# Second sums made in the bank of the first, evictions ahead of statistics, and output stores on another queue

## The chip, the cores and the metric

The kernel runs on one core of one Trainium2 chip. Its time is the device time of an execution in microseconds. Before the change it was 1675.91 us, the median of three runs (1675.52 to 1676.21). One more execution was taken by the hardware profiler; all positions below are microseconds from the start of its span.

## What is computed

Four layers on a sequence of 2048 tokens with 512 features: spectral, attention, spectral, attention. Each adds its result to x. The two spectral layers are alike, and so are the two attention layers.

```python
def spectral(x, w_r, w_i):
    X = rfft2(x.astype(float32))           # over tokens s and features d
    return irfft2(X * (w_r + 1j * w_i), s=(2048, 512)).astype(bfloat16)

def attention(x, wq, wk, wv, wo):          # 32 heads of 16, one shared k and v
    q = (x @ wq).reshape(B, S, 32, 16).transpose(0, 2, 1, 3)
    k, v = x @ wk, x @ wv
    p = softmax(einsum("bhqd,bkd->bhqk", q, k) / 4)
    return einsum("bhqk,bkd->bhqd", p, v).transpose(0, 2, 1, 3).reshape(B, S, 512) @ wo

for layer in (spectral, attention, spectral, attention):
    x = x + layer(layernorm(x))
```

## The kernel before, in words

**State.** `x_sb` and its normalised copy `xn_sb` stay in SBUF as 16 blocks of 128 tokens by 512 features, block (r, t) with r and t from 0 to 3. `k = 4t + r` numbers the blocks in the closing loops.

**Spectral layer** (`spectral_layer`, L201). The transforms are matrix products with tables of cosines and sines. `over_s` sums over tokens into `G` (for the third layer most of it is done at the end of the attention layer before, by `sequence`), DVE combines the four residues t into `X` (L231 to L242), and `over_d` (L262) sums over features. For a half c of the frequencies it is called with sign 0 and with sign 1: the first result is a + b, the second a - b, where a is the sum with the cosines and b with the sines, per real and imaginary part and for two blocks of frequencies. Each call has four results, and each result is eight matmuls into a PSUM bank of its own (L275) and an eviction by ACT into `F`, which lies in the buffer of `xn_sb` (L279). The table `DT` holds cos, sin and -sin. Then DVE multiplies by the weights (`times_w`, L293 to L295), combines the signs (`combine`, L299 to L318) into `st`, and TensorE goes back over d (L367) and over s (L379). A few frequencies left over go another way (`extras`, L320): small matmuls with `DT` (L325, L326), one copy by ACT (L329), a row of small operations on POOL (L335 to L353), and a copy by DVE into `st[0]` (L410). In the first layer alone `prepare_w` brings the weights into the layout `WT` (TensorE L151 and L153, ACT L158, DVE L160), and POOL copies the raw `wq` (L882).

**Order of the spectral stage** (L400 to L424): sums over d for c = 0, sign 0 and 1; weights; sums for c = 1, sign 0; extras; products of c = 0; sums for c = 1, sign 1; back over d; and so on.

**Attention layer** (`attention_layer`, L497). A written-out loop of steps feeds ACT's exponentials (L669), a share of them made on DVE (L693, L699), and the sums over keys (L681). The function `chain` makes each of TensorE, ACT, DVE and POOL keep the order in which the program text issues; the SP queue, which issues every DMA, is not among those four.

**Its end** (L742 to L823). The output product of the 16 blocks runs in triples of blocks, each triple in a PSUM tile of three banks (two such tiles exist, pool `psc`), and four last blocks which wait for the last group of heads. `finish` (L650) adds a block to x: where `with_x` holds, TensorE adds x by a product with the identity and ACT copies the result (L653); else DVE adds (L655). In the layer between (`nxt` set), `statistics` (L742, L743) and `normal` (L749 to L758) make the next layer's normalised blocks, and `sequence` starts its sums over tokens (L192), evicted by ACT (L197). In the last layer each finished block is stored to DRAM (L891).

The last group's denominators take a way of their own: `evict` copies the sums to SBUF (L584), writes one row per head to DRAM (`d`, L586) and reads it back spread over partitions (`den`, L588); `invert` takes the reciprocal (L592), writes it (L594) and reads it back broadcast, in four DMAs (`rb`, L597). Then POOL multiplies (`od`, L619), and TensorE adds the last product of the four last blocks.

Of the kernel before, what the change touches and what calls it, by code (L numbers as in the profile page):

```python
# [11 lines left out]
P = 128  # L12
# [6 lines left out]
NC = 4  # L19
# [23 lines left out]
def host_tables():  # L43
# [24 lines left out]
    tabs["DT"] = bf(np.stack([np.cos(angd), np.sin(angd), -np.sin(angd)], axis=2))  # L68
# [132 lines left out]
def spectral_layer(nc, tc, tabs, shared, lnpool, x_sb, xn_sb, WT, WX, aw, nxt, loads):  # L201
# [5 lines left out]
    with (tc.tile_pool(name="workA", bufs=1) as work,  # L207
# [54 lines left out]
        def over_d(c, sign, by_half):  # L262
            pss = [None] * 4
            for bs in ((0, 1), (2, 3)) if by_half else ((0, 1, 2, 3),):
                for i in range(4):
                    fb, comp = divmod(i, 2)
                    if pss[i] is None:
                        pss[i] = psum.tile([P, 512], F32, tag="pa", name=f"fd{i}")
                    for b in bs:
                        for part in range(2):  # L270
                            if part == comp:
                                w = 0
                            else:
                                w = 1 if (part == 1) == (sign == 0) else 2
                            nc.tensor.matmul(pss[i], lhsT=DT[:, b, w, 128 * fb:128 * fb + 128],  # L275
                                             rhs=X[:, b, part, c, :, :].rearrange("p k j -> p (k j)"),
                                             start=(b == 0 and part == 0), stop=(b == 3 and part == 1))
                    if bs[-1] == 3:
                        nc.scalar.copy(out=F[:, 8 * c + 4 * comp + 2 * fb + sign, :], in_=pss[i])  # L279

        Z = work.tile([P, 2, 2, 2, 512], BF, name="Z")
        V = work.tile([P, 2, 2, 2, 4, 128], BF, name="V")
# [117 lines left out]
        over_d(0, 0, True)  # L400
        over_d(0, 1, False)
# [4 lines left out]
        over_d(1, 0, False)  # L406
# [4 lines left out]
        over_d(1, 1, False)  # L411
# [85 lines left out]
def attention_layer(nc, tc, tabs, shared, lnpool, x_sb, xn_sb, aw, prep, nxt, store):  # L497
    with ExitStack() as ctx:
# [151 lines left out]
        def finish(k, ps, with_x):  # L650
            t, r = divmod(k, 4)
            if with_x:
                nc.scalar.copy(out=x_sb[:, r, t, :], in_=ps)  # L653
            else:
                nc.vector.tensor_tensor(out=x_sb[:, r, t, :], in0=ps, in1=x_sb[:, r, t, :], op=ALU.add)  # L655
            if store is not None:
                store(r, t)
# [64 lines left out]
        mv, n_x = {}, 1 if nxt is None else 2  # L722

        def triple(i):
            ps = psc.tile([P, 3, 512], F32, tag="sc", name="tri")
            for j in range(3):
                outproj(3 * i + j, ps[:, j, :], j < n_x)
            return ps

        def triple_out(i, ps):  # L730
            for j in range(3):
                finish(3 * i + j, ps[:, j, :], j < n_x)

        def statistics(ks):
            if nxt is None:
                return
            for k in ks:
                t, r = divmod(k, 4)
                if r == 0:
                    mv[t] = lnpool.tile([P, 4, 2], F32, tag="ln_mv4", bufs=4, name="mv")  # L740
                stats = lnpool.tile([P, 6], F32, tag="ln_stats", bufs=4)
                nc.vector.bn_stats(stats, x_sb[:, r, t, :])  # L742
                nc.vector.bn_aggr(mv[t][:, r, :], stats)  # L743

        def normal(t):
            if nxt is None:
                return
            rstd = lnpool.tile([P, 4], F32, tag="ln_rstd4", bufs=4)
            nc.scalar.activation(out=rstd, in_=mv[t][:, :, 1], func=ACT.Sqrt, bias=tabs["eps"], scale=1.0)  # L749
            nc.vector.reciprocal(rstd, rstd)  # L750
            nb = lnpool.tile([P, 4], F32, tag="ln_nb4", bufs=4)
            nc.vector.scalar_tensor_tensor(out=nb, in0=mv[t][:, :, 0], scalar=-1.0, in1=rstd, op0=ALU.mult, op1=ALU.mult)
            for r, eng in ((0, nc.scalar), (1, nc.gpsimd), (2, nc.vector), (3, nc.vector)):
                x_ap, xn_ap = x_sb[:, r, t, :], xn_sb[:, r, t, :]
                if eng is nc.scalar:
                    eng.activation(out=xn_ap, in_=x_ap, func=ACT.Identity, bias=nb[:, r:r + 1], scale=rstd[:, r:r + 1])
                else:
                    eng.tensor_scalar(out=xn_ap, in0=x_ap, scalar1=rstd[:, r:r + 1], scalar2=nb[:, r:r + 1],  # L758
                                      op0=ALU.mult, op1=ALU.add)
# [34 lines left out]
        normal(0)  # L794
        triple_out(2, p2)
        normalise(NG - 1, o, rb)
        if nxt is not None:
            nxt["load"](2)
        p3 = triple(3)
        statistics((6, 7, 8))  # L800
        normal(1)
        triple_out(3, p3)
# [5 lines left out]
        for i in range(4):  # L808
            outproj(12 + i, pf[i], i % 2 == 0)
        statistics((9, 10, 11))  # L810
        normal(2)
        q0 = sequence(0)
        sequence_out(q0)
        for i in range(4):
            outproj(12 + i, pf[i], False, last_group=True)
# [5 lines left out]
        normal(3)  # L821
# [7 lines left out]
def full_kernel(ctx, tc, A_x, A_w_r, A_w_i, B_x, B_wq, B_wk, B_wv, B_wo, out,  # L829
# [39 lines left out]
    def late_loads(work):  # L869
        wq_raw = work.tile([P, NC, D], BF, name="wq_raw")  # L870
# [19 lines left out]
    def store(r, t):  # L890
        nc.sync.dma_start(out=out_v[:, r, t, :], in_=x_sb[:, r, t, :])  # L891
# [62 lines left out]
```

## Time and profile before

| | |
|---|---|
| median of three runs | 1675.91 us |
| the profiled execution | 1673.17 us |
| its span, first to last instruction | 1671.4 us |
| mean granted TensorE clock | 0.977 |
| busy in the span: PE, DVE, ACT, POOL | 85%, 93%, 90%, 9% |
| DMA: moved, share of 16 engines (hardware queue) | 40.26 MB, 7.7% |
| first spectral layer and attention's inputs | about 0 to 132 us |
| attention loop of layer 2 | about 132 to 820 us |
| end of layer 2, third layer | about 820 to 957 us |
| attention loop of layer 4, tail | about 957 to 1645 us, 1645 to 1671.4 us |

A row of a timeline has the start, the time from first to last of a run of like instructions, the engine, the line, the operation, output <- inputs, shapes, how many, and in brackets the idle time of that engine before it with what ended it. "SPq" is the SP queue, which issues DMAs. The chain view has the start, the length and what the path that ended last was doing.

### The profile page before, as it was taken

The page shows a single profiled execution, that of the slowest core. Times are in us where ns is not written, and L with a number is a line of the kernel's source. Part 1 is how long each engine was busy: PE and PEld are TensorE (multiplying, and loading weights), DVE is VectorE, ACT ScalarE, POOL GpSimd, SP SyncE. Part 2 cuts the span into 40 slices and gives each one's busy share as a digit, 9 for nine tenths or more (in the row PEclk, how much of TensorE's full clock was granted, in tenths as well). Part 3 has the DMA queues.
Part 4 walks back from the last instruction along what each step waited for, and adds up shares of the span by engine and source line. Part 5 has one row for each costly group of instructions (what it writes and reads, how often), then busy time and mean ns, then how long its engine had stood idle before and what let it go on. Part 6 is the DMA issues. An engine that isn't in the chain of part 4 may idle for free.

```text
span 1671.4 us, 32246 instructions
## 1 busy us (share of the span) xinstructions
PE 1421.6 (85%) x12756; PEld 459.7 (28%) x12756; DVE 1551.7 (93%) x2796; ACT 1505.6 (90%) x1250; POOL 158.4 (9%) x264
## 2 busy tenths in 40 slices
PE   7889888888888888888988798888888888888887
PEld 2331222222222222222333322222222222222222
DVE  6877999999999999999878689999999999999994
ACT  4358999999999999999843699999999999999994
POOL 3210000000000000000111100000000000000000
PEclk9896999999999999999999789999999999999999
DMA  7000000000000010000020000000000000000002
GB/s 276 2 1 4 14 16 17 17 16 17 17 17 16 16 29 16 17 17 28 24 70 1 1 8 17 17 16 17 17 16 16 17 15 15 14 16 17 16 17 65
DMA packets 47880, 40.26 MB, mean 24 GB/s; under 512 B 30832, under 2 KB 36208, under 8 KB 47472
## 3 DMA queue, kind: packets, MB, share of 16 engines
q1 hardware_dynamic: 47728, 38.19, 7.7%
q8 instruction: 100, 1.64, 0.4%
q14 instruction: 52, 0.43, 0.1%
HBM read 33.04 MB, written 3.15 MB: 22 GB/s over the span
## 4 chain that ended last, share of the span: by engine, by line
DVE 39%; ACT 24%; PE 18%; issue 17%; DMA 1%; POOL 1%; SPq 0%; POOLq 0%; DVEq 0%; ACTq 0%
ACT e L669 23%; DVE t_new L693 15%; DVE s_new L699 12%; PE pv_new L681 6%; PE dv L569 3%; PE sc L569 2%; DVE o L584 2%; DVE qt L446 2%; PE fd L275 2%; DVE qt L447 2%; PE ps L192 1%; DVE stats L125 1%; PE ps L367 1%; PE ps L379 1%; DVE den L592 1%
## 5 line engine op out<-in xcount | busy, mean ns | idle before, releaser
L669 ACT ACTIVATE e<-sc 128x1536 bf16<-128x1536 f32 (+1 forms) x1028 | 1386.4, 1526 | 16.0 <-PE sc L569 15.5
L693 DVE TENSOR_SCALAR t_new<-dv 128x512 int16<-128x512 f32 x1016 | 695.0, 684 | 35.8 <-PE sc L569 14.5
L699 DVE TENSOR_SCALAR s_new<-t_new 128x2048 int16<-128x2048 int16 x1016 | 698.3, 688 | 0.0
L569 PE MATMUL dv<-qt,KT 32*128 32x512 bf16 x1016 | 389.2, 383 | 121.8 <-DVE t_new L693 114.0
L569 PE MATMUL sc<-qt,KT 32*128 32x512 bf16 x3080 | 421.6, 389 | 36.5 <-ACT e L669 3.2
L681 PE MATMUL pv_new<-s_new,vaug 128*32 128x512 bf16 x4064 | 412.0, 393 | 27.0 <-DVE qt L446 27.0
L681 PE MATMUL pv_new<-e,vaug 128*32 128x512 bf16 x3080 | 408.7, 385 | 0.4 <-ACT e L669 0.4
L569 PEld LDWEIGHTS <-KT 32*128 32x128 bf16 x4096 | 201.2, 91 | 730.1 <-issue 714.9
L681 PEld LDWEIGHTS <-vaug 128*32 128x32 bf16 x7144 | 135.6, 94 | 276.1 <-issue 262.5
L625 POOL TENSOR_TENSOR ot_new<-o,rb 128x176 bf16<-128x176 f32 (+1 forms) x96 | 55.7, 582 | 706.8 <-DVE s_new L699 649.9
L625 POOL TENSOR_TENSOR od<-o,rb 128x176 bf16<-128x176 f32 (+1 forms) x90 | 49.6, 551 | 597.6 <-DVE s_new L699 597.6
L441 PE MATMUL ps<-xT,wq_sb 128*128 128x512 bf16 x256 | 66.3, 381 | 10.8 <-DVE o L584 10.8
L275 PE MATMUL fd<-X,tab_DT 128*128 128x512 bf16 x256 | 56.1, 379 | 2.8 <-DVE X L242 2.8
L279 ACT CAST xn_sb<-fd 128x512 bf16<-128x512 f32 x32 | 18.8, 586 | 40.7 <-PE fd L275 40.7
L446 DVE CAST qt<-ps 128x512 bf16<-128x512 f32 x64 | 44.2, 691 | 0.8 <-PE ps L441 0.8
L584 DVE COPY o<-pv_new 128x512 f32<-128x512 f32 x64 | 43.8, 684 | 0.1
L367 PE MATMUL ps<-tab_PS,st 128*128 128x512 bf16 x128 | 32.8, 416 | 13.0 <-DVE st L315 12.0
L373 ACT CAST U<-ps 128x512 bf16<-128x512 f32 x24 | 14.1, 587 | 29.8 <-PE ps L367 29.8
L125 DVE BATCH_NORM_STATS2 stats<-x_sb 128x6 f32<-128x512 bf16 x48 | 31.8, 677 | 7.2 <-ACT x_sb L383 3.7
L441 PEld LDWEIGHTS <-wq_sb 128*128 128x128 bf16 x256 | 24.6, 96 | 39.7 <-issue 16.0
L275 PEld LDWEIGHTS <-tab_DT 128*128 128x128 bf16 x256 | 24.8, 98 | 32.8 <-issue 3.6
L379 PE MATMUL ps<-U,IT 128*128 128x512 bf16 x128 | 33.2, 379 | 0.0
(133 smaller groups left out, 567.2 us busy)
## 6 DMA issues: line engine op xcount, KB each, us to landing
rb<-d SPq DMA_DIRECT2D x256, 64.0 KB
FT<-const_FT SPq DMA_DIRECT2D x8, 512.0 KB
IT<-const_IT SPq DMA_DIRECT2D x8, 512.0 KB
x_sb<-in_A_x_dram SPq DMA_DIRECT2D x4, 512.0 KB
out_dram<-x_sb SPq DMA_DIRECT2D x16, 128.0 KB
ot_new<-od SPq DMA_DIRECT2D x120, 16.0 KB
wr_raw<-in_A_w_r_dram SPq DMA_DIRECT2D x1, 1028.0 KB
wi_raw<-in_A_w_i_dram SPq DMA_DIRECT2D x1, 1028.0 KB
```

The costliest lines, as they stand in the source:

```text
L275: nc.tensor.matmul(pss[i], lhsT=DT[:, b, w, 128 * fb:128 * fb + 128], rhs=X[:, b, part, c, :, :].rearrange("p k j -> p (k j)"), start=(b = ...
L367: nc.tensor.matmul(ps, lhsT=st[c][:, t, vec, q, fb, :], rhs=PS[:, fb, w, :], start=(k == 0), stop=(k == 3))
L379: nc.tensor.matmul(ps, lhsT=IT[:, t, part, c, r * P:(r + 1) * P], rhs=U[:, t, part, c, :], start=(k == 0), stop=(k == 3 and r % 2 == 1))
L441: nc.tensor.matmul(ps, lhsT=wq_sb[:, c, hg, :], rhs=xTq[qb][:, c, :], start=(c == 0), stop=(c == NC - 1))
L446: nc.vector.tensor_copy(out=qt, in_=ps)
L569: nc.tensor.matmul(dst, lhsT=KT[hs, kc * P:(kc + 1) * P], rhs=QT[g][hs, :], start=True, stop=True)
L584: nc.vector.tensor_copy(out=o, in_=pv.pop(g))
L625: pace(nc.gpsimd.tensor_tensor(out=dst[:, a:b], in0=o[:, a:b], in1=rb[:, a:b], op=ALU.mult))
L669: nc.scalar.activation(out=e[:, 0:na, :], in_=sc[:, 0:na, :], func=ACT.Exp, scale=SCALE)
L681: nc.tensor.matmul(pv[g][32 * h:32 * h + 32, :], lhsT=vaug[:, max(j, 0), kc, :], rhs=rhs, start=(first_pv[(g, h)] == u), stop=(last_pv[(g, ...
L693: nc.vector.tensor_scalar(out=tb[(g, kc // 4)][:, kc % 4, :], in0=dv, scalar1=T_MUL, scalar2=T_ADD, op0=ALU.mult, op1=ALU.add)
L699: image[0] = nc.vector.tensor_scalar(out=s_new, in0=tb[(g, b)], scalar1=0.5, scalar2=16384.0 + PH_OFF[j], op0=ALU.mult, op1=ALU.add)
```

## The change

1. `over_d` makes both sums of a pair. The four banks of the first sums are kept; for the second, TensorE adds four products with -2 sin or 2 sin into the bank from which ACT has just copied the first. `DT` holds five tables instead of three, and `V` and `wq_raw` now share a buffer, one waiting for the other.
2. At the end of the attention layer that has a next one, the evictions of triple 2 come ahead of `normal(0)`, those of triple 3 ahead of the statistics of triple 2 and of `normal(1)`; `normal` is split so that the square root on ACT can be issued earlier than the rest; the fourth block's normalisation goes from DVE to ACT.
3. In the last layer no block of the first twelve goes by way of the identity product and ACT: DVE adds them all. Of the 16 stores, 14 are issued on POOL's queue, and two (blocks 13 and 15) on SP's.

```diff
@@ host_tables
-    tabs["DT"] = bf(np.stack([np.cos(angd), np.sin(angd), -np.sin(angd)], axis=2))
+    tabs["DT"] = bf(np.stack([np.cos(angd), np.sin(angd), -np.sin(angd), 2 * np.sin(angd), -2 * np.sin(angd)], axis=2))
@@ before L259, after L259
 
         F = xn_sb.rearrange("p r t d -> p (r t) d")
 
-        def over_d(c, sign, by_half):
+
+        def over_d(c, by_half):
             pss = [None] * 4
+
+            def add(i, b, part, w, start, stop):
+                fb = i // 2
+                nc.tensor.matmul(pss[i], lhsT=DT[:, b, w, 128 * fb:128 * fb + 128],
+                                 rhs=X[:, b, part, c, :, :].rearrange("p k j -> p (k j)"),
+                                 start=start, stop=stop, skip_group_check=True)
+
+            def out(i, sign):
+                fb, comp = divmod(i, 2)
+                nc.scalar.copy(out=F[:, 8 * c + 4 * comp + 2 * fb + sign, :], in_=pss[i])
+
             for bs in ((0, 1), (2, 3)) if by_half else ((0, 1, 2, 3),):
                 for i in range(4):
-                    fb, comp = divmod(i, 2)
+                    comp = i % 2
                     if pss[i] is None:
                         pss[i] = psum.tile([P, 512], F32, tag="pa", name=f"fd{i}")
                     for b in bs:
                         for part in range(2):
-                            if part == comp:
-                                w = 0
-                            else:
-                                w = 1 if (part == 1) == (sign == 0) else 2
-                            nc.tensor.matmul(pss[i], lhsT=DT[:, b, w, 128 * fb:128 * fb + 128],
-                                             rhs=X[:, b, part, c, :, :].rearrange("p k j -> p (k j)"),
-                                             start=(b == 0 and part == 0), stop=(b == 3 and part == 1))
+                            add(i, b, part, 0 if part == comp else 1 + comp, b == 0 and part == 0, b == 3 and part == 1)
                     if bs[-1] == 3:
-                        nc.scalar.copy(out=F[:, 8 * c + 4 * comp + 2 * fb + sign, :], in_=pss[i])
+                        out(i, 0)
+            yield
+            for i in range(4):
+                comp = i % 2
+                for b in range(4):
+                    add(i, b, 1 - comp, 4 - comp, False, b == 3)
+                out(i, 1)
 
         Z = work.tile([P, 2, 2, 2, 512], BF, name="Z")
-        V = work.tile([P, 2, 2, 2, 4, 128], BF, name="V")
+        V = work.tile([P, 2, 2, 2, 4, 128], BF, tag="V", bufs=1, name="V")
@@ before L397, after L409
         slots()
-        over_d(0, 0, True)
-        over_d(0, 1, False)
+        f0 = over_d(0, True)
+        next(f0)
+        next(f0, None)
         if raw:
             prepare_w(nc, tabs, psum, raw, WT, WX)
         times_w(0, 0, lo)
         times_w(0, 0, hi)
-        over_d(1, 0, False)
+        f1 = over_d(1, False)
+        next(f1)
         rx = extras()
         times_w(0, 1, both)
         combine(st[0], both)
         v.tensor_copy(out=st[0].rearrange("p t v q m j -> p t (v q) m j")[:, :, 1:3, :, 0], in_=rx)
-        over_d(1, 1, False)
+        next(f1, None)
         back_d(0)
         times_w(1, 0, both)
@@ before L654, after L668
             else:
                 nc.vector.tensor_tensor(out=x_sb[:, r, t, :], in0=ps, in1=x_sb[:, r, t, :], op=ALU.add)
             if store is not None:
-                store(r, t)
+                store(r, t, nc.sync if t == T - 1 and r % 2 == 1 else nc.gpsimd)
@@ before L719, after L733
-        mv, n_x = {}, 1 if nxt is None else 2
+        mv, n_x = {}, 0 if nxt is None else 2
@@ before L744, after L758
 
         def normal(t):
             if nxt is None:
-                return
+                return lambda: None
             rstd = lnpool.tile([P, 4], F32, tag="ln_rstd4", bufs=4)
             nc.scalar.activation(out=rstd, in_=mv[t][:, :, 1], func=ACT.Sqrt, bias=tabs["eps"], scale=1.0)
-            nc.vector.reciprocal(rstd, rstd)
-            nb = lnpool.tile([P, 4], F32, tag="ln_nb4", bufs=4)
-            nc.vector.scalar_tensor_tensor(out=nb, in0=mv[t][:, :, 0], scalar=-1.0, in1=rstd, op0=ALU.mult, op1=ALU.mult)
-            for r, eng in ((0, nc.scalar), (1, nc.gpsimd), (2, nc.vector), (3, nc.vector)):
-                x_ap, xn_ap = x_sb[:, r, t, :], xn_sb[:, r, t, :]
-                if eng is nc.scalar:
-                    eng.activation(out=xn_ap, in_=x_ap, func=ACT.Identity, bias=nb[:, r:r + 1], scale=rstd[:, r:r + 1])
-                else:
-                    eng.tensor_scalar(out=xn_ap, in0=x_ap, scalar1=rstd[:, r:r + 1], scalar2=nb[:, r:r + 1],
-                                      op0=ALU.mult, op1=ALU.add)
+
+            def rest():
+                nc.vector.reciprocal(rstd, rstd)
+                nb = lnpool.tile([P, 4], F32, tag="ln_nb4", bufs=4)
+                nc.vector.scalar_tensor_tensor(out=nb, in0=mv[t][:, :, 0], scalar=-1.0, in1=rstd,
+                                               op0=ALU.mult, op1=ALU.mult)
+                for r, eng in ((0, nc.scalar), (1, nc.gpsimd), (2, nc.vector), (3, nc.scalar)):
+                    x_ap, xn_ap = x_sb[:, r, t, :], xn_sb[:, r, t, :]
+                    if eng is nc.scalar:
+                        eng.activation(out=xn_ap, in_=x_ap, func=ACT.Identity, bias=nb[:, r:r + 1],
+                                       scale=rstd[:, r:r + 1])
+                    else:
+                        eng.tensor_scalar(out=xn_ap, in0=x_ap, scalar1=rstd[:, r:r + 1], scalar2=nb[:, r:r + 1],
+                                          op0=ALU.mult, op1=ALU.add)
+            return rest
 
         def sequence(first):
             if nxt is None:
@@ before L791, after L810
         rb = invert(den)
         p2 = triple(2)
         statistics((3, 4, 5))
-        normal(0)
         triple_out(2, p2)
+        rest = normal(0)
+        p3 = triple(3)
+        rest()
         normalise(NG - 1, o, rb)
         if nxt is not None:
             nxt["load"](2)
-        p3 = triple(3)
+        triple_out(3, p3)
         statistics((6, 7, 8))
-        normal(1)
-        triple_out(3, p3)
+        rest = normal(1)
         if nxt is not None:
             nxt["load"](3)
         ps_a = psc.tile([P, 3, 512], F32, tag="sc", name="tri")
@@ before L807, after L827
         pf = [ps_a[:, 0, :], ps_a[:, 1, :], ps_a[:, 2, :], ps_b]
         for i in range(4):
             outproj(12 + i, pf[i], i % 2 == 0)
+        rest()
         statistics((9, 10, 11))
-        normal(2)
         q0 = sequence(0)
         sequence_out(q0)
+        rest = normal(2)
+        rest()
         for i in range(4):
             outproj(12 + i, pf[i], False, last_group=True)
         for i in range(4):
@@ before L818, after L840
         q1 = sequence(3)
         statistics((12, 13, 14, 15))
         sequence_out(q1)
-        normal(3)
+        rest = normal(3)
+        rest()
         for first in (6, 9):
             q2 = sequence(first)
             sequence_out(q2)
@@ before L867, after L890
         return raw
 
     def late_loads(work):
-        wq_raw = work.tile([P, NC, D], BF, name="wq_raw")
+        wq_raw = work.tile([P, NC, D], BF, tag="V", bufs=1, name="wq_raw")
         nc.sync.dma_start(out=wq_raw, in_=B_wq.rearrange("(c p) j -> p c j", p=P))
         wk_v = B_wk.rearrange("(c p) j -> p c j", p=P)
         for i in range(8):
@@ before L887, after L910
     out_v = out_flat.rearrange("(r p t) d -> p r t d", r=R, p=P, t=T)
     n_layers = len(layers)
 
-    def store(r, t):
-        nc.sync.dma_start(out=out_v[:, r, t, :], in_=x_sb[:, r, t, :])
+    def store(r, t, eng):
+        eng.dma_start(out=out_v[:, r, t, :], in_=x_sb[:, r, t, :])
```

## The prediction, made before the changed kernel was run

> **What bounds the kernel now.** I read the busy shares first, then the chain that ended last, then the timelines of the stretches that the change touches. The chain spends most of the span in the two attention loops (about 132 to 820 us and 957 to 1645 us), which the change leaves alone. What it can move lies in four stretches, each with its own limit: the spectral stage of the first layer, the end of the first attention layer, the spectral stage of the third layer, and the tail.
>
> In the first stage, the chain (start, length, what) goes from TensorE's sums over d straight to the preparation of W:
> ```profile
> 29.41 13.97 PE fd L275 x64
> 43.38 0.03 PE ps L151
> ...
> 43.88 3.69 DVE WT L160 x6
> ```
> DVE stood idle for 4.15 us before 43.88, so TensorE sets the time there. But not by much: DVE's earlier work ended late, beside a POOL copy.
> ```profile
> 33.68 1.86 DVE L250 TENSOR_TENSOR uv<-G 128x4 f32<-128x4 bf16 x1
> ...
> 37.35 1.88 DVE L252 SCALAR_TENSOR_TENSOR Y<-uv,G 128x4 bf16<-128x4 f32 x1
> ...
> 39.57 0.17 DVE L257 COPY Y<-Y 128x16 bf16<-128x16 bf16 x1
> ```
> ```profile
> 31.22 7.98 POOL L882 COPY wq_sb<-wq_raw 128x2048 bf16<-128x2048 bf16 x2 [12.91 <-DMA wq_raw<-in_B_wq_dram]
> ```
> Two tiny DVE operations of 128x4 took 1.86 and 1.88 us where their like take 0.15 and 0.17; both end with one of the two POOL copies (35.5 and 39.2).
>
> In the third layer DVE waits three times; in brackets, its idle time and what ended it:
> ```profile
> 876.38 0.69 DVE L293 TENSOR_TENSOR m<-xn_sb,WT 128x1024 bf16<-128x1024 bf16 x1 [1.44 <-ACT xn_sb L279]
> ...
> 878.17 0.69 DVE L294 TENSOR_TENSOR m<-xn_sb,WT 128x1024 bf16<-128x1024 bf16 x1 [1.09 <-ACT xn_sb L279]
> ...
> 892.48 0.21 DVE L410 COPY st<-rx 128x16 bf16<-128x16 bf16 x1 [1.05 <-POOL rx L353]
> ```
> The first two are for the second sums' evictions, the third for POOL's small operations, which start after TensorE's extra sums at 884. From 892.48 to the next TensorE stage at 905.90 the chain is DVE alone.
>
> At the end of the first attention layer the chain runs through statistics on DVE and evictions on ACT:
> ```profile
> 853.91 0.31 ACT rstd L749
> ...
> 854.72 0.81 ACT xn_sb L756
> 855.53 2.94 ACT G L197 x6
> 858.47 0.04 issue
> 858.51 1.90 PE ps L192 x8
> ```
> In the tail, one denominator travels d, den, d, rb through DRAM on the SP queue, between stores of the output:
> ```profile
> 1651.18 0.55 SPq L586 DMA_DIRECT2D d<-o  x1
> 1652.71 1.06 SPq L891 DMA_DIRECT2D out_dram<-x_sb  x2
> 1653.86 0.38 SPq L588 DMA_DIRECT2D den<-d  x1
> ...
> 1660.18 1.79 SPq L597 DMA_DIRECT2D rb<-d  x4
> 1662.02 7.01 SPq L891 DMA_DIRECT2D out_dram<-x_sb  x6
> ...
> 1663.98 1.26 POOL L619 TENSOR_TENSOR od<-o,rb 128x512 bf16<-128x512 f32 x1 [21.24 <-DMA rb<-d]
> ```
> Everything after waits for od at 1665.24.
>
> **Part 1, sums over d.** A pair took 64 matmuls and takes 48: 16 fewer, four pairs in all. A second sum must wait until ACT has read the first from its bank. That wait has cover: the eviction lasts 0.59 us, and 12 or more matmuls (2.6 us) lie between it and the next write to that bank. I cost it at nothing.
>
> *First layer.* A matmul takes 13.97 / 64 = 0.218 us, so W's preparation starts 16 x 0.218 = 3.5 us earlier: DVE could cast at 43.88 - 3.5 = 40.4. Next late is DVE itself. The table DT grows from 768 to 1280 KB; the DMA engines were full (392 to 423 GB/s between 10 and 25 us), so all loads queued behind DT land 0.52 MB / 0.41 MB per us = 1.3 us later, among them wq_raw, for which POOL's copies wait. If the two held DVE operations move with them, DVE is free at 39.74 + 1.3 = 41.0. Gain 43.9 - 41.0 = 2.8 (3.5 if they don't). W's raw tables were there before 31 us, so 1.3 us more is covered. After that DVE is gapless to the end of the stage, so the second pair's 16 matmuls bring nothing. [...] The buffer that V now shares with wq_raw adds a wait on POOL's copies; they end at about 40.5 and V is first written after 54, so nothing.
>
> *Third layer.* At 20.88 / 96 = 0.2175 us a matmul, the second sums of the first pair end at 863.48 + 48 x 0.2175 = 873.9, the last eviction at 874.6, before DVE is free (874.94). So the idles of 1.44 and 1.09 go: 2.5 us. TensorE's extra sums come 3.5 us earlier, POOL starts at 881.7; its chain of 7.3 us would end at 889.0, when DVE, now at 888.9, needs it: gain 892.5 - 889.0 = 3.5. Beside a busier DVE POOL is slower: in the first layer the same chain took 10.2 us, which would leave 0.5. The pairing with DVE's operations shifts by only 0.9 us, so I stay near the upper end: 3.1. DVE's gapless run carries it to the end of the stage.
>
> **Part 2, the first attention layer's end.** The last add and ACT's evictions of triples 2 and 3 now come ahead of normalisation and statistics, and one of four normalisations moves from DVE (0.37 us) to ACT (0.76 us). Following the queues: ACT evicts triple 2 at 832.9 to 833.9, the four normalisations follow at 835.6, triple 3's evictions end at 838.2 instead of 842.7, TensorE's first sequence runs from 839.8 instead of 843.5. Then ACT is the limit: two normalisations, three evictions of G, rstd, two normalisations, the closing evictions from 847.1 instead of 848.75; statistics end at 852.2 instead of 853.9, 1.7 us sooner; then one normalisation more on ACT stands ahead of the six evictions (0.76). Gain 1.7 - 0.8 = 0.9, between 0 (ACT slips further) and 1.7.
>
> **Part 3, the tail.** Two changes: all of the first 12 blocks are added on DVE (one TensorE product with the identity and one ACT copy fewer per triple), and 14 of 16 stores leave the SP queue for POOL's. Triple 0 ends at 1648.4 instead of 1648.6; three adds at 0.61 follow without an ACT copy before them; o is evicted by 1650.9 (1651.15). Without stores, the hops take what they take at 828 to 832: 1.71 from d to den, 1.70 to the reciprocal (before: 2.68 and 4.01), at 1654.4. DVE's order lets it in, since triple 1's adds end at 1653.4. Then 0.28 + 1.8 (between 1.6 at 164 and 2.0 here) + 3.8 for rb: od can start at 1660.3 and end at 1661.5, 3.7 us sooner; the last ACT copy at 1664.5.
> But POOL runs in order: nine stores stand ahead of od and five behind. No row shows a store issued from POOL. Call its cost c. Rows near it: SP issues the same store in 0.33 us; POOL's 128x512 operations take 0.78 to 1.27. I take c = 1.0, as POOL's work on a tile of this shape; ends 0.33 and 1.3. The nine are done at 1649.1 + 9 = 1658.1, before rb lands. Behind od: 1661.5 + 5 = 1666.5, and 2.37 us from the last issue to the end, as before (1669.03 to 1671.4): 1668.9, a gain of 2.5. In general the end is 1663.9 + 5c, and from c = 1.24 on 1652.7 + 14c, since then the nine delay od. At 0.33 the last copy sets it: gain 4.2; at 1.3 it is 0.5. [...]
>
> **Sum.** 2.8 + 3.1 + 0.9 + 2.5 = 9.3 us. The profiled execution took 1673.17 (span 1671.4 and 1.8 around it), 2.7 below the median of the runs shown. 1673.17 - 9.3 = 1663.9; set on the median, 1675.91 - 9.3 = **1666.6**.
>
> **Rivals.**
> 1. *POOL's stores are somewhat dearer* (c from 1.24 to 1.82): od waits for them, and 14c counts. At 1.5 the tail loses 2.3, the total gain is 4.5: 1671.4. For it: POOL's slow rows (1.18 us for 128x4). Against: no arithmetic is done.
> 2. *POOL is held until each store has landed*: the side slower. Price c = 2.37, the way from the last issue to the end: 1652.7 + 33.2 = 1685.9, 14.5 lost, 7.7 net: 1683.6. It turns the sign from c = 1.82. Against: SP's queue does not hold (three stores in 1.66 us).
> 3. *POOL's small operations stay slow in the third layer*: 0.5 instead of 3.1, 1669.2. For it the first layer's 10.2 us.
> 4. *DVE holds POOL's stores*: the stores of a triple then start when its adds are through (1650.9, 1653.4, 1656.6); with c = 1 the nine end at 1659.6, still before rb. The result is the forecast's 1666.6. [...]
>
> **How the numbers follow.** Forecast (with 4) 0.66; rival 1 0.15; rival 2 0.08; rival 3 0.11. A measurement can tell about 0.2%, 3.4 us. Faster by more: 0.66 + 0.11 + 0.08 of rival 1 (c up to 1.57) = 0.85; within: the other 0.07 of rival 1; slower: 0.08. Range: the best ends (3.5, 3.5, 1.7, 4.2) give 12.9 off, 1663.0; I set 1662.5. Above, up to c = 1.68 in rival 1: 1674.0. Left out: rival 2, 0.04 of rival 1 and 0.04 below.
>
> **What would show it.** L275's successor with 192 matmuls and no new TensorE wait; WT's first cast near 41; the idles of 1.44, 1.09 and 1.05 gone; TensorE's sums after the pool change near 0.9 us earlier against the loop's end; the reciprocal at about 9 us after the last exp's end instead of 12.6; POOL's stores near 1 us each and od started by rb, not by a store. It is wrong if POOL reaches od after rb, if DVE waits anew for second sums, or if POOL's chain grows as DVE fills.

## The result, and the profile after

The changed kernel took 1662.24 us, the median of four runs (1658.68 to 1666.36), beside 1675.72 for the kernel before in the same series; the ratio is 0.9922 (95% interval 0.9898 to 0.9946). Forecast were 1666.6 us and a range of 1662.5 to 1674.0. The sign was right, and the gain was larger than forecast: 13.1 us by the ratio instead of 9.3, a little more than the 12.9 that the prediction's four best ends give. Set on the forecast's own base of 1675.91, the ratio gives 1662.8 us, just inside the range; the plain median lies 0.3 us below it. A second series (below) gave 0.9931 (0.9917 to 0.9945). The profiled execution took 1662.98 us, its span 1661.2. Cut at the same events in both traces, the span divides so:

| stretch, us | before | after | difference | forecast |
|---|---|---|---|---|
| start to W's first cast | 43.88 | 40.27 | -3.61 | -2.8 |
| to the first layer's second `back_d` | 36.20 | 36.42 | +0.22 | 0 |
| to the first exp of layer 2 | 43.98 | 41.82 | -2.16 | 0 |
| loop of layer 2, to the last exp's end | 699.91 | 700.69 | +0.78 | 0 |
| to TensorE's sums after the pool change | 34.54 | 33.02 | -1.52 | -0.9 |
| to the third layer's sums over d | 4.97 | 4.98 | 0 | 0 |
| to the third layer's second `back_d` | 42.42 | 39.30 | -3.12 | -3.1 |
| to the first exp of layer 4 | 42.85 | 43.01 | +0.16 | 0 |
| loop of layer 4 | 697.84 | 699.57 | +1.73 | 0 |
| tail | 24.81 | 22.12 | -2.69 | -2.5 |

The four forecast terms came to 10.9 us; the loops and what leads into them, which were forecast to stand still, moved by up to 2.2 us each, in both directions.

The timeline of the changed kernel's first layer, with the lines that answer to L250, L252, L257 and POOL's copies of before:
```profile
32.56 6.48 POOL L905 COPY wq_sb<-wq_raw 128x2048 bf16<-128x2048 bf16 x2 [14.37 <-DMA wq_raw<-in_B_wq_dram]
...
33.52 1.87 DVE L250 TENSOR_TENSOR uv<-G 128x4 f32<-128x4 bf16 x1
...
37.20 1.87 DVE L252 SCALAR_TENSOR_TENSOR Y<-uv,G 128x4 bf16<-128x4 f32 x1
...
39.41 0.17 DVE L257 COPY Y<-Y 128x16 bf16<-128x16 bf16 x1
...
40.27 4.88 DVE L160 CAST WT<-ps 128x512 bf16<-128x512 f32 x8 [0.70 <-PE ps L153]
```
The copies start 1.34 us later than before (32.56 instead of 31.22), as forecast from the longer load. Yet the two held operations stand where they stood, and DVE is free at 39.58. W's cast waits only 0.70 us for TensorE, instead of 4.15.

The timeline of DVE in the third layer:
```profile
868.57 0.69 DVE L305 TENSOR_TENSOR m<-xn_sb,WT 128x1024 bf16<-128x1024 bf16 x1
869.17 0.69 DVE L306 TENSOR_TENSOR m<-xn_sb,WT 128x1024 bf16<-128x1024 bf16 x1
...
883.08 0.21 DVE L424 COPY st<-rx 128x16 bf16<-128x16 bf16 x1 [0.62 <-POOL rx L365]
```
No bracket stands behind the first two lines any more (1.44 and 1.09 before), and the wait for POOL's chain is 0.62 instead of 1.05.

The end of the first attention layer, from the timeline:
```profile
846.95 0.30 ACT L763 ACTIVATE rstd<-mv,eps 128x4 f32<-128x4 f32 x1 [1.69 <-DVE mv L757]
...
847.75 1.52 ACT L773 ACTIVATE xn_sb<-x_sb,nb,rstd 128x512 bf16<-128x512 bf16 x2 [0.50 <-DVE nb L768]
...
849.17 3.00 ACT L197 CAST G<-seq 128x512 bf16<-128x512 f32 x6
...
852.22 1.02 PE L192 MATMUL ps<-FT,xn_sb 128*128 128x512 bf16 x4 [3.05 <-ACT G L197]
```
ACT now normalises twice (1.52) ahead of its six evictions, but its rstd comes 27.75 us after the last exp's end instead of 29.94.

The tail, from the timeline:
```profile
1647.46 0.25 DVE L606 RECIPROCAL den<-den 128x16 f32<-128x16 f32 x1 [1.42 <-DMA den<-d]
...
1648.55 1.73 POOL L914 DMA_DIRECT2D out_dram<-x_sb  x3 [1.67 <-DVE x_sb L669]
1649.16 1.71 SPq L611 DMA_DIRECT2D rb<-d  x4
...
1653.27 1.25 POOL L633 TENSOR_TENSOR od<-o,rb 128x512 bf16<-128x512 f32 x1 [2.99 <-DMA rb<-d]
...
1656.90 0.59 ACT L667 CAST x_sb<-tri 128x512 bf16<-128x512 f32 x1 [0.81 <-DVE x_sb L669]
1657.77 0.54 POOL L914 DMA_DIRECT2D out_dram<-x_sb  x1 [0.86 <-ACT x_sb L667]
```
Three stores take POOL 1.73 us; one by one, 13 of the 14 took 0.54 to 0.58 us and the first 0.75. That is the prediction's c. POOL waits 2.99 us for rb, no store is in its way. The reciprocal stands 8.4 us after the last exp's end (11.3 before). The prediction's 9 and 12.6 fit a count from 1.3 us ahead of that end; its 1654.4 is 7.8 us after it, so the reciprocal came 0.6 us later than forecast.

### The profile page after: what moved, and what is told of

It reads as the page before. It is cut to its first block, busy times and chain, and to the rows that moved or that the text cites. A ratio compares the mean times of both kernels' runs of the same rounds, so it can differ in the third digit from the quotient of the medians.

```text
span 1661.2 us, 32022 instructions
## 1 busy us (share of the span) xinstructions
PE 1404.5 (85%) x12606; PEld 453.6 (27%) x12688; DVE 1549.5 (93%) x2796; ACT 1506.4 (91%) x1250; POOL 164.6 (10%) x278
## 3 DMA queue, kind: packets, MB, share of 16 engines
q0 software_dynamic: 672, 1.84, 0.3%
## 4 chain that ended last, share of the span: by engine, by line
DVE 39%; ACT 24%; PE 17%; issue 17%; DMA 1%; POOL 1%; DVEq 0%; SPq 0%; POOLq 0%; ACTq 0%
ACT e L683 23%; DVE t_new L707 15%; DVE s_new L713 12%; PE pv_new L695 6%; PE dv L583 3%; DVE o L598 2%; PE sc L583 2%; DVE qt L460 2%; PE fd L268 2%; DVE qt L461 2%; DVE stats L125 1%; PE ps L391 1%; PE ps L379 1%; DVE den L606 1%; PE ps L192 1%
## 5 line engine op out<-in xcount | busy, mean ns | idle before, releaser
L695 PE MATMUL pv_new<-s_new,vaug 128*32 128x512 bf16 x4064 | 413.3, 394 | 27.3 <-DVE qt L460 27.3
L455 PE MATMUL ps<-xT,wq_sb 128*128 128x512 bf16 x196 | 62.3, 378 | 13.9 <-DVE o L598 10.7
L379 PE MATMUL ps<-tab_PS,st 128*128 128x512 bf16 x126 | 34.1, 433 | 17.1 <-DVE st L327 13.9
L268 PE MATMUL fd<-X,tab_DT 128*128 128x512 bf16 x186 | 41.9, 379 | 3.1 <-DVE X L242 2.8
L192 PE MATMUL ps<-FT,xn_sb 128*128 128x512 bf16 x79 | 20.0, 406 | 14.4 <-ACT xn_sb L134 10.9
```

The source lines that it names most:

```text
L379: nc.tensor.matmul(ps, lhsT=st[c][:, t, vec, q, fb, :], rhs=PS[:, fb, w, :], start=(k == 0), stop=(k == 3))
L455: nc.tensor.matmul(ps, lhsT=wq_sb[:, c, hg, :], rhs=xTq[qb][:, c, :], start=(c == 0), stop=(c == NC - 1))
L695: nc.tensor.matmul(pv[g][32 * h:32 * h + 32, :], lhsT=vaug[:, max(j, 0), kc, :], rhs=rhs, start=(first_pv[(g, h)] == u), stop=(last_pv[(g, ...
```

## The experiments

Eleven more runs were made, one of them of the changed kernel again. Three things needed proof: whether each part brings what the trace says, what holds DVE, and what the stores are worth. One more thing nobody had forecast: why loops that the change leaves alone take another time.

**The parts alone, and the whole again.** The same chip ran each hunk of the diff by itself on the kernel before, and the changed kernel once more.

> Part 1 alone (second sums by -2b, the longer DT, V on wq_raw's buffer) on the kernel before. Theory (TensorE's 16 matmuls per pair, and DVE not held later by POOL's copies): W's first cast near 40.3 us instead of 43.9, back_d of the first layer near 76.7 instead of 80.1, third layer another 3.1 us; together 6.7 us, 1669.0. If the dip of TensorE's granted clock at 80 to 85 us of the kernel before belongs to the order of its work and part 1 moves it away, the first exp of layer 2 is near 118.5 and the total gain 8.9 us, 1666.8. Rival (the dip falls by chance and not by the edit): the first exp is near 120.7 with a dip between 76 and 100 us, and 1669.0. By the forecast on record (DVE held 1.3 us later): first cast at 41.0, total gain 5.9, 1669.8.

> Part 2 alone (evictions ahead of statistics, fourth normalisation on ACT) on the kernel before. Theory: from the end of the attention loop of layer 2 to TensorE's sums after the pool change 1.5 us less (as in the changed kernel's trace), nothing elsewhere: 1674.2. By the forecast on record 0.9 less: 1674.8. Rival (the gain of the changed kernel's trace there is only clock): 0.0 to 0.5, 1675.2 to 1675.7. The dip of the granted clock at 80 to 85 us should stand as in the kernel before if it belongs to the order of the work, since nothing before 820 us differs.

> Part 3 alone (all twelve first blocks added on DVE; 14 of 16 stores on POOL's queue) on the kernel before. Theory: reciprocal 8.4 us after the last exp's end instead of 11.3, stores 0.55 to 0.6 us each on POOL, never ahead of od; tail 2.7 us shorter, 1673.0. By the forecast on record (1.0 us a store) 2.5, 1673.2. Rival (only the changed clock of the changed kernel's tail, .91, made it that long): 3.7, 1672.0. The dip at 80 to 85 us stands as in the kernel before.

> The changed kernel once more, on the same chip as its three parts. Theory (parts add, 8.9 + 1.5 + 2.7): 13.1 us, 1662.6, with no dip of the granted clock between 76 and 92 us; its runs spread by some 7 us, and longer runs have a lower mean clock, the difference lying in the first 75 us of the two attention loops. Rival (the 2.2 us between 80 and 124 us were chance): this profile shows the dip there again, and a first exp near 120.7.

Measured, beside 1674.0 us (21 runs, 1670.49 to 1676.14):

| | median, us | ratio (95%) | W's cast | first exp | loop 2 | after loop 2 | third layer | loop 4 | tail |
|---|---|---|---|---|---|---|---|---|---|
| part 1 | 1666.11 | 0.9955 (0.9943 to 0.9968) | 40.12 | 121.04 | 696.82 | 34.62 | 39.30 | 699.76 | 23.64 |
| part 2 | 1671.53 | 0.9992 (0.9981 to 1.0002) | 43.73 | 122.95 | 696.82 | 33.12 | 42.42 | 697.18 | 24.90 |
| part 3 | 1669.65 | 0.9982 (0.9971 to 0.9994) | 43.68 | 121.56 | 698.33 | 34.74 | 42.42 | 697.02 | 22.95 |
| all | 1660.24 | 0.9931 (0.9917 to 0.9945) | 40.40 | 118.37 | 698.00 | 33.02 | 39.30 | 699.53 | 21.98 |

The parts add: 0.9955 x 0.9992 x 0.9982 = 0.9929. Each part's stretch moves by the same amount wherever the part is in, to 0.3 us, and not where it is out; only the tail scatters by 1 us. In the whole time part 2 does not stand out (its interval includes 1); its own stretch shows it. The dip of the granted clock that the expectations ask about comes and goes by chance: of three kernels that are the same up to 820 us (before, parts 2 and 3), only the kernel before has half a clock at 81.3 to 84.7 us, on TensorE's path; part 1 alone has one at 77.4 to 80.9 and reaches the first exp at 121.04, and the changed kernel has none in either profile. The stretch that ends with the first exp took 41.6 to 44.5 us in these six profiles, with no order by part. So its 2.16 us are chance, not the change's. But loop 4 lasts 699.5 to 699.8 with part 1 in all three profiles, and 697.0 to 697.8 without it: part 1 gives back some 2.3 us there.

**Is it the early start?** In these six profiles the half clock at loop 4's start ended 144 to 150 us after the end of loop 2, which suggests a set time. In this kernel `combine` gets `times`, 20 in one call of the third layer and 1 elsewhere.

```diff
-            for vec, op in enumerate((ALU.add, ALU.subtract)):
+            for vec, op in enumerate((ALU.add, ALU.subtract) * times):
+                vec = vec % 2
```

> The changed kernel with 38 needless operations of 128x512 on DVE, which write the same sums again, in the third layer's stretch where DVE alone is the path (some 13 us by the pace of 0.34 of their like). It asks what an us ahead of the fourth layer's attention loop is worth. Theory (in six profiles TensorE's granted clock came back to full 144 to 150 us after the end of the first attention loop, whatever lay between, so a loop that starts later has less of itself at half clock; an us at half clock cost the loop about 0.42 us): first exp 13 us later, loop 4 shorter by 0.42 x 13 = 5.5 us (694 instead of 699.6), total +7.5 us against the changed kernel. Rival (the half clock follows the loop's own start): loop 4 stays at 699.6 and the total is +13 us.

Measured: 1689.18 us, ratio 1.0103 (1.0082 to 1.0124), against 1662 for the changed kernel: 27 us by the medians and 29 to 30 by the ratios, not 7.5 and not 13. The operations turned out twice as large as taken (40 in 24.2 us), so the third layer's stretch grew by 23.1; loop 4 grew too, to 702.0. My theory falls: the half clock does not end at a set time. But the profile shows a spell at half clock, and its end (each line: the stretch, its length, the busy time and number of instructions of PE, PEld, DVE, ACT and POOL, the granted clock, the DMA share and GB/s):
```profile
885.00:891.50 6.50, 4.13 (x20) 1.67 (x17) 6.47 (x11) 3.36 (x6) 0.00 (x0) 1.00 0.00 0
891.50:912.30 20.80, 0.02 (x1) 0.02 (x2) 20.80 (x40) 0.00 (x0) 0.00 (x0) 0.50 0.00 0
912.30:915.40 3.10, 2.72 (x6) 0.66 (x6) 3.03 (x9) 0.00 (x0) 0.00 (x0) 0.50 0.00 0
915.40:920.00 4.60, 2.69 (x12) 1.29 (x14) 3.54 (x11) 1.17 (x2) 0.00 (x0) 1.00 0.00 0
```
TensorE is busy for 0.02 of 20.80 us and its clock is half; behind a stretch of 3.1 us with six full-size matmuls (128 rows and 128 columns of the array) it is full again.

**Can the loops be kept at full clock?** In the lines above the half clock ended behind 2.72 us of full-size matmuls. At the start of a loop of the changed kernel it lasted through 28.7 us (15.33 + 13.40) of small ones:
```profile
110.40:113.80 3.40, 1.20 (x10) 0.77 (x12) 0.97 (x3) 1.85 (x4) 0.00 (x0) 1.00 0.00 0
113.80:117.20 3.40, 1.09 (x18) 0.68 (x16) 2.04 (x7) 0.94 (x3) 0.00 (x0) 0.50 0.02 5
118.50:134.50 16.00, 15.33 (x80) 2.20 (x79) 10.09 (x16) 14.27 (x10) 0.00 (x0) 0.50 0.00 0
134.50:147.90 13.40, 13.40 (x77) 2.08 (x73) 7.06 (x11) 9.97 (x8) 0.00 (x0) 0.50 0.00 1
```
TensorE was busy for 15.33 of 16 us, then for all of 13.4, and stayed at 0.50; ACT, which bounds the loop later on (busy for all of 300 to 600 us), is busy 9.97 of 13.4. Scores use 32 rows of the array (32*128 in the trace) and sums over keys 32 columns (128*32). The theory was that such matmuls do too little work in the array to bring the clock back. So the test put matmuls of full size there, 27 in TensorE's gaps before the loop (by calls of `warm` in the attention inputs) and three in each of the loop's first six steps:

```diff
+        def warm(n):
+            if n:
+                ps = psum.tile([P, 512], F32, tag="pa")
+                for _ in range(n):
+                    nc.tensor.matmul(ps, lhsT=aw["wo"][:, 0, 0:P], rhs=aw["wo"][:, 0, :], start=True, stop=True)
...
+            if n < 6:
+                for i in range(len(act_tiles[n])):
+                    nc.tensor.matmul(sc[:, i, :], lhsT=wo_sb[:, 0, 0:P], rhs=wo_sb[:, 0, :], start=True, stop=True)
```

> The changed kernel with 45 needless 128x128 by 512 matmuls per attention layer: 27 in TensorE's gaps of the last 12 us before the loop (where the trace shows it idle for 0.8 to 2.5 us at a time), 18 ahead of the scores of the first six steps (their results are overwritten by the scores). In every profile so far TensorE's clock falls to half after a stretch in which it does little, and at each loop's start it stays at half for 20 to 30 us although TensorE is then busy all the time, with matmuls of 32 rows or 32 columns only. Theory (the clock follows the amount of work done in the array, not the busy time; the loop, once at half clock, does too little to come out of it): with the gaps filled, the clock stays full or comes back within 10 us of the first exp; loop 2 falls from 698.5 to about 690 and loop 4 from 699.6 to 690 (ACT stood idle for 6 us in the first 36 us of loop 2 beyond its later pace; 0.42 us per us at half clock, over 20 to 27 us, gives 8 to 11), less some 1 to 2 us by which the needless matmuls delay scores: total -10 to -16 us, 1646 to 1652. Rival (half clock at the loop's start has another cause, such as a limit on a sudden load): dips stay, and the time rises by 0 to 4 us.

> The kernel before with the same 45 needless matmuls per attention layer. Theory (part 1 gives back 2.3 us in loop 4, since loop 4 stayed at half clock for 27.5 us after its first exp with part 1 in seven profiles, and for 21 to 23 without it in three): with both loops warm, loop 4 lasts the same with and without part 1, and the changed kernel's lead in the profiles' stretches is the sum of the stages alone: 3.3 + 3.1 + 1.5 + 2.0 to 2.8, about 10 us. Rival (loop 4's loss is not the clock's): loop 4 is 2 us shorter here than in the changed kernel with the same matmuls.

Measured: the changed kernel 1657.03 us, ratio 0.9893 (0.9862 to 0.9924), its profiled run 1649.19; the kernel before 1662.25, ratio 0.9944 (0.9923 to 0.9965). The same windows of the changed kernel with these matmuls:
```profile
110.40:113.80 3.40, 3.40 (x23) 1.50 (x21) 1.21 (x4) 2.08 (x4) 0.00 (x0) 1.00 0.02 5
113.80:117.20 3.40, 1.67 (x22) 0.79 (x20) 2.09 (x7) 0.94 (x3) 0.00 (x0) 1.00 0.00 0
118.90:134.90 16.00, 15.46 (x113) 4.50 (x113) 12.05 (x20) 15.20 (x12) 0.00 (x0) 1.00 0.01 1
134.90:148.30 13.40, 11.07 (x94) 3.39 (x97) 10.40 (x18) 13.34 (x11) 0.00 (x0) 1.00 0.00 1
```
In this profile the clock did not fall ahead of either loop, and it stayed full: ACT was busy 13.34 of 13.4, and loop 2 and loop 4 took 693.4 us each, 3 more than the 690 of the theory. Other runs went otherwise: the five took 1649.2 and 1650.8 us at a mean granted clock of 0.993, 1657.0 and 1658.5 at 0.987 and 0.988, and 1664.5 at 0.981. Their interval overlaps that of the changed kernel (0.9922 and 0.9931), so a gain on top of it is not shown by the medians. For the kernel before, the gain is clear of the noise. The profiled run of that kernel (1674.90) shows the limit. Its clock fell to half at 121.5 us, behind a window in which TensorE was busy for 1.49 of 3.4 us. These are windows of that run (two) and of the last run of this section, which has the same matmuls (one):
```profile
118.10:121.50 3.40, 1.49 (x7) 0.40 (x5) 2.63 (x8) 0.58 (x3) 0.00 (x0) 1.00 0.00 0
121.50:135.20 13.70, 13.70 (x47) 2.58 (x47) 4.93 (x8) 7.25 (x5) 0.00 (x0) 0.50 0.00 0
...
118.50:121.90 3.40, 3.40 (x14) 0.67 (x10) 1.38 (x2) 2.33 (x2) 0.00 (x0) 0.50 0.00 0
```
Of the 47 matmuls in the second line 15 are of full size, about four in a window of 3.4 us, and the clock stayed at half up to 159.1; its loop 2 took 708.0 us. In the third line six of 14 are of full size, and the clock was full again behind it. And once the clock is full, it stays so in the loop with almost nothing but small matmuls (1101 of 1119 from 165 to 300 us in the changed kernel, at 1.00). So what worked was to enter the loop at full clock; that the work in the array is what counts is not shown, and the second line speaks against a simple form of it.

Loop 4 of the same profile kept the full clock and took 693.6, as long as with part 1. So in this pair of profiles the loss of 2.3 us in loop 4 is the clock's, against the rival. The changed kernel's lead, both with these matmuls, is 5.2 us by the medians of all runs; in the runs with a mean clock of at least 0.992 it is 1662.0 - 1650.0 = 12.0 us (seven runs and two), where 10 were expected. Why the half clock lasts 6 us longer into loop 4 with part 1 (to 27.3 to 27.6 us after its first exp in six profiles; to 20 to 22 in the three without, one of which had 3.4 us more of it later; 33.9 in all in the delayed kernel) stays open.

**What holds DVE.** wq_raw's load was put behind those of the other weights.

```diff
-        nc.sync.dma_start(out=wq_raw, in_=B_wq.rearrange("(c p) j -> p c j", p=P))
         wk_v = B_wk.rearrange("(c p) j -> p c j", p=P)
...
+        nc.sync.dma_start(out=wq_raw, in_=B_wq.rearrange("(c p) j -> p c j", p=P))
         for half in range(2):
             nc.gpsimd.tensor_copy(
```

> The changed kernel with wq_raw loaded after the other weights of the attention layer instead of ahead of them, so that POOL's two copies start later. Theory (DVE's run of bf16 operations keeps POOL's copy out until an operation of another kind comes; then the copy runs 1.8 us and DVE's operation waits that long; so each copy holds DVE once, and when it started does not matter): if the copies start between 34 and 37 us, the first of the two 128x4 operations takes 0.15 us, the second still 1.87, and the slots end near 37.8 instead of 39.6; if they start after 37.4, neither is held and the slots end at 36. Rival (as in the forecast on record: DVE is held until the copies end, so a later copy moves the end): the slots end later than 39.6 by as much as the copies start later. By neither does the total change much, since TensorE's sums set W's first cast at 40.3: 0 to +1 us.

Measured: 1672.52 us, ratio 0.9999 (0.9986 to 1.0012): all of the gain gone. From the timeline:
```profile
33.44 0.16 DVE L250 TENSOR_TENSOR uv<-G 128x4 f32<-128x4 bf16 x1
...
35.40 0.17 DVE L252 SCALAR_TENSOR_TENSOR Y<-uv,G 128x4 bf16<-128x4 f32 x1
```
and from the view of the tile `wq_sb` (shortest, median and longest copy in ns; who waited for it, us, times):
```profile
L905 POOL COPY wq_sb<-wq_raw x2: 1887/1888/1890, 57.0 to 58.8; 128x2048 bf16<-128x2048 bf16 x2
...
  DVE V L311: 5.3, 1
```
The copies came at 57, far later than thought. Neither operation was held, and the operations of `slots` (those that answer to L250 to L257) ended at 36.08: the theory's second case. A copy alone takes 1.89 us, close to a hold (1.87 less 0.15 of its own work). So DVE's operation waits for about one whole copy, and before it the copy waits for DVE: in the changed kernel the two copies took 2.81 and 3.72 us, 0.92 and 1.83 more than alone; the held operations started 0.96 and 1.88 us after them, and each copy ended within 0.03 us of the end of one. The cost was mispriced, 0 to 1 us: V shares its buffer with wq_raw, DVE waited 5.3 us for the copies, and the second `back_d` came at 82.31 instead of 76.7. The other half of the 10 us is not on this path; loop 2 and the stretches before the two loops were at the long end (699.9, 43.9, 44.7).

**What the stores are worth, and a shorter tail.**

```diff
-                store(r, t, nc.sync if t == T - 1 and r % 2 == 1 else nc.gpsimd)
+                store(r, t, nc.sync)
```

> The changed kernel with all 16 stores on SP's queue again; the first blocks are still all added on DVE. Theory (the stores' place gives nearly all of the tail's gain: the three hops of the denominator stand behind stores on SP): the tail from the last exp's end to the end is 23.4 to 24.7 us instead of 22.1, +1.3 to +2.6 us. Rival (the twelve adds on DVE, which free the first hop 0.24 us earlier and spare ACT, give it): 22.4 at most, +0.3 us.

Measured: 1662.55 us, ratio 0.9943 (0.9923 to 0.9964); tail 22.37. The rival is right: with all stores on SP the tail is only 0.2 us longer (one profile each). The reads of rb stood behind stores (issued 2.16 us after the reciprocal's write, 1.42 with POOL's stores) and od started 0.8 us later; but the end came 3.2 us after the last copy instead of 3.7. Stores on POOL have a price too: od started 2.1 to 3.2 us after the last read of rb was issued in the eight profiles that have them, and 1.7 to 2.0 us in the five with all stores on SP. And the hops scatter: with the stores on SP and the old adds, the hop from den's read to the reciprocal took 4.01, 1.98, 2.01 and 2.08 us, and the tail 24.8, 23.6, 24.9 and 23.1 (before, part 1, part 2, before with the matmuls). So the stores' place alone does not explain the second and worst delay in the profile before, since it was the same in all four.

```diff
-                nc.gpsimd.tensor_tensor(out=dst, in0=o, in1=rb, op=ALU.mult)
+                (nc.vector if nxt is None else nc.gpsimd).tensor_tensor(out=dst, in0=o, in1=rb, op=ALU.mult)
...
-                store(r, t, nc.sync if t == T - 1 and r % 2 == 1 else nc.gpsimd)
+                store(r, t, nc.sync if t == T - 1 else nc.gpsimd)
```
`normalise` stands behind `triple_out(3, p3)` in the last layer here. The second kernel has the full-size matmuls as well.

> The changed kernel with two further edits in the tail: the last denominator's product od on DVE instead of POOL, put behind DVE's adds of the fourth triple, and the four last stores all on SP's queue. Theory: od takes 0.7 instead of 1.26 us (0.5 less), and the end comes 2.4 to 3.2 us after the last copy as with SP's stores before, instead of 3.7 (0.5 less): tail 21.0 to 21.2 instead of 22.1. [...]

> Both improvements on the changed kernel: od on DVE and the last stores on SP (its tail measured 21.0 us instead of 22.1), and the needless matmuls that should keep TensorE's clock up. Theory: 1.1 us less than the changed kernel with those matmuls, 1645 to 1651. Rival (the tail's 1.1 us are lost in the whole time, whose median was 1665.3 for the tail's edit alone): no less than it.

Measured: the tail took 20.96 us, the theory's sum, though not by its terms: od started 0.3 us sooner and took 0.69, and the end came 3.5 us after the last copy, not 2.4 to 3.2. The lines:
```profile
1654.02 0.69 DVE L633 TENSOR_TENSOR od<-o,rb 128x512 bf16<-128x512 f32 x1 [1.71 <-DMA rb<-d]
...
1656.29 2.20 SPq L916 DMA_DIRECT2D out_dram<-x_sb  x4
```
The whole took 1665.27 us, ratio 0.9958 (0.9939 to 0.9977), no better than the changed kernel; 1.1 us are less than the spread between runs. With the full-size matmuls as well it took 1652.56 us, ratio 0.9885 (0.9854 to 0.9915), the lowest median of all, but its interval overlaps that without the tail's edit (0.9893), and its tail was 22.02 this time, since rb landed later. That the tail's edit helps the whole time is not shown.

## Why the prediction was right, and where it was not

**First layer.** The 16 matmuls were sized well: W's cast moved by 3.61 us in the profiles, and by 3.3 to 3.6 in the others. The step that failed is "If the two held DVE operations move with them, DVE is free at 39.74 + 1.3 = 41.0". They didn't move. A hold (1.87 us, less 0.15 of the operation's own work) has about the length of one copy alone (1.89), and where it falls goes with DVE's own run of operations: the copies began at 31.22 us before and at 32.56 after, yet L250 started at 33.68 and 33.52 and L252 at 37.35 and 37.20. Until then the copy waited: it took longer than alone by 2.42 and 1.84 us before and by 0.92 and 1.83 after, to 0.05 us the time from its start to that of the held operation. What DVE did in that time was not slowed (L240 0.42 us and L242 0.28 to 0.29, beside the copies as in the third layer). Why the copy waits through a whole row of instructions, and why it goes ahead at L250 and L252, no run told. That the second sums' wait costs nothing held: TensorE's longest new wait within the sums is 0.05 us, and the sums took 0.22 us a matmul as before. So did the cover of V's wait on the copies, with 15 us to spare; the late load showed what it costs when that cover is gone.

**Third layer.** 3.12 us measured, 3.1 forecast, and 2.8 to 3.1 in every profile with part 1 but the delayed one. POOL's chain took 7.6 us in the changed kernel, near the 7.3 that was chosen, and far from the 10.2 of rival 3.

**End of the attention layer.** The mechanism held, the size was 0.6 too small: ACT's last rstd came 2.2 us sooner instead of 1.7, and the second normalisation cost 0.67 instead of 0.76. Part 2 alone gave 34.54 - 33.12 = 1.4 us there, so it is not the clock's.

**Tail.** 2.69 us measured against 2.5, but by two errors that cancel. A store costs POOL 0.55 us, not 1.0; at so low a cost the prediction had a gain of about 4.2, with the last copy setting the end. But od started 0.5 us later than taken, and the last store on POOL ended 0.82 us after the last copy and landed 2.9 after that, 3.7 together where 0.33 + 2.37 = 2.7 had been taken. So the sum came out near by luck. Over all profiles the tail gained about 24.1 - 22.2 = 1.9 us (means of four and six profiles), and the stores' move itself no more than a few tenths; the adds on DVE brought most of it, as far as one profile tells. Rivals 1, 2 and 4 did not come; against 4, the first three stores began at 1641.92 us, before DVE's three adds ended at 1642.81.

**What was left out.** The prediction put the two attention loops, "which the change leaves alone", at no difference. That is the step that was wrong beyond the stretches: their length goes with TensorE's granted clock at their start, which varies from run to run and, in loop 4, is lower for longer with part 1 (half to 27.3 to 27.6 us after the first exp, beside 20 to 22). The four terms came to 10.9 us in the profiled pair, and with the 2.16 ahead of the first exp, where the profile before happened to have a half clock, less 2.5 in the loops and 0.4 elsewhere, this makes its 10.2. By the ratios the gain is 11.6 to 13.1; the last us or two can't be put down to a place, since loop 2 alone took 696.8 to 700.8 in the ten profiles without added matmuls.

## What to carry to other kernels

Price a gain on TensorE with the clock in mind: look at the granted clock of the stretch behind the gain as well as at the gain. Where a stage of small matmuls starts at half clock, it can pay to keep the clock from falling with some full-size ones in the gaps ahead of it. Here loops took 3 to 7 us less where that worked, and it brought the kernel before nearly as much as the whole change (ratio 0.9944 beside 0.9922 and 0.9931). But it did not work in every run: in one profile the clock was at half for 38 us all the same, and that loop took at least 7 us more than any loop 2 without them. And when an operation of one engine takes long and ends with another engine's, set the hold beside the other's instruction alone (here 1.72 and 1.89 us), and see what both engines did ahead of it, before pricing a move: the copies started 1.34 us later here, and the held operations stayed.

## What the runs showed of the hardware

- TensorE's granted clock was 0.5 or 1.0. Before and after the change its spells at half lasted 3.4, 6.8, 10.2, 27.3, 34.1 and 37.5 us (those that the end of the span does not cut short). It fell behind stretches with little matmul work (TensorE busy for 0.00 and 1.20 of 3.4 us in the changed kernel, 1.49 in the kernel before with the full-size matmuls) and came back in the delayed kernel after 3.1 us with six 128x128 matmuls, but at a loop's start it stayed at 0.5 for 20 to 31 us from the first exp on, with TensorE busy for 15.33 of 16 and all of 13.4 us with matmuls of 32 rows or columns; yet with 1101 such matmuls among 1119 it stood at 1.00 from 165 to 300 us. So busy time alone does not set it. That the work in the array does is not shown: 15 full-size matmuls among small ones in 13.7 us left it at 0.50, and six in 3.4 us brought it back. No threshold was measured.
- The spread of the times goes with it: five runs of one kernel went from 1649.2 us at a mean clock of 0.993 to 1664.5 at 0.981.
- A 128x512 store took POOL 0.54 to 0.58 us to issue, the first 0.75; on SP one took 0.33 to 0.42 in the kernel before and 0.36 in the changed one.
- POOL's copy of 128x2048 took 1.89 us alone (late load), and two took 6.48 to 7.98 beside DVE's work (before, after, part 1); in all three profiles two DVE operations of 128x4 took 1.86 to 1.88 us beside them, and 0.16 and 0.17 without.
